# Zero rows that fill the packed remainder of the gate/up products from 96 to 128 rows

## The chip, the cores and the metric

The kernel runs on one core of a Trainium2 chip. A core has five engines that work on their own and meet through semaphores: TensorE (PE, matmuls; PEld is its weight load), VectorE (DVE), ScalarE (ACT), GpSimd (POOL) and SyncE (SP, which only issues transfers here). Each takes its instructions in the order in which the program puts them. The metric is the time of one execution on the device in microseconds; lower is better.

## What is computed

One transformer block over 2048 tokens of 576 features, in float32. The second half, which the change touches, is a gated feed-forward part with 4608 hidden features:

```python
def _B_ref(x, w_gate, w_up, w_down):
    g = _silu(x @ w_gate)
    u = x @ w_up
    return (g * u) @ w_down

h = _layernorm(x, axis=-1) * (1 + ca) + sa
x = x + ga * _A_ref(h, A_wq, A_wk, A_wv, A_wo, A_beta)
h = _layernorm(x, axis=-1) * (1 + cb) + sb
x = x + gb * _B_ref(h, B_w_gate, B_w_up, B_w_down)
```

`_A_ref` is an attention with 32 heads of 18 features in four segments of 512 tokens, with a memory between segments and the output projection `o @ wo`. The factors `sa` to `gb` come from a small product with the vector `c`.

## The kernel before

**Precision.** A float32 operand is split into a high part that the array takes exactly (`wh`, written by a cast on ACT, L1166) and the rest (`wl`, a subtraction on DVE, L1167). A product is then three matmuls: high by high, low by high, high by low.

**Gate and up.** The feed-forward part runs twice over 1024 tokens (`t`), each time over 18 pairs of hidden tiles (`p`), and for each pair over gate and up (`z`). Such a block, 2 x 2 tiles with 512 tokens, 288 features and 128 hidden features a tile, is formed with seven products instead of eight, on sums and differences of the operands: `y[:, o]` holds the seven activation operands (o from 0 to 6), `O` the seven weight operands (three loaded, four formed by `sum_o`, L1157). That makes 2 x 18 x 2 x 7 = 504 products, each written by `prod` (L1195 to L1203) into one of the PSUM banks A, B, C.

A product has 288 = 2 x 128 + 32 contracted features. The two full blocks take three matmuls each. The 32 left over are packed: `R[z]` (tile `wr`) holds on partitions 0 to 31 the high part, on 32 to 63 the low part, on 64 to 95 the high part again, and `y[:, o, 4]` the high, high and low part. So one matmul over 96 partitions does all three. It is the seventh and last of its product. `prep_r` fills `wr`: at `t` 0 with a cast on ACT (L1151) and a subtraction on DVE (L1152), in two parts (slots 0 to 2 and 3 to 6); at `t` 1 with a load of what `store_r` had kept in DRAM. The activations' packed rows are written by `y_here` or loaded by `load_y`.

**Down.** Between the products PE does the down product of the pair before (`down` L1306, `plain` L1323), six or twelve matmuls of 288 columns at a time.

**The order.** Everything after the attention is written under a manual schedule: each engine's instructions stand as the loops write them. `later` is a list of subtractions that `flush` puts on DVE one step after their casts on ACT. The change lies in the stage between the attention and the feed-forward loop. There PE does the output projection of the last segment, `wo_m` (L729, `pw`): 4 token blocks (i) by 2 halves (h), each half 14 matmuls in 4 portions (c), numbered n = 8 i + 4 h + c. Two PSUM banks take turns for the halves, and `wo_x` (L734, `xr`, on DVE) empties one. Beside these portions the first feed-forward operands are made at fixed n: the lists `SS` (sums `sum_o`, the first four on POOL, the last four on DVE), `HH` (`y_here`) and `WW` (`prep_r` and `prep_w`). Ahead of them POOL forms `ys` (`y_sum`, L1037). Afterwards the loop starts with a load of `wd` (L1174) and of the operand 3 of `y` (L1122), both on SP's queue.

The sums in the order that `SS` gives, and the packed matmul:

```python
d, a, b, op = ((4, 3, 2, ALU.add), (5, 4, 0, ALU.subtract), (3, 0, 3, ALU.subtract), (6, 1, 5, ALU.subtract))[j]
eng.tensor_tensor(o[:, d], o[:, a], o[:, b], op=op)

ops.append((R[z][0:96, SLOT[m]], y[0:96, o, 4]))
```

Of the kernel before, what the change touches and what calls it, by code (L numbers as in the profile page):

```python
# [8 lines left out]
F32R = mybir.dt.float32r  # L9
# [6 lines left out]
P = 128  # L16
# [51 lines left out]
def f32(ap):  # L68
    return ap.bitcast(F32)
# [3 lines left out]
def block(ctx: ExitStack, tc: tile.TileContext, x, wqk, wv, wo, beta, wgu, wd, c, w_mod, out):  # L73
    nc = tc.nc
    def pool(stk, name, bufs=1, **kw):
        return stk.enter_context(tc.tile_pool(name=name, bufs=bufs, reuse_waits="tile", **kw))
# [167 lines left out]
    with ExitStack() as p1:  # L244
# [211 lines left out]
        def proj(s, t):  # L456
            hh, hl, hr = hT[s]
            pp = ps.tile([P, L], F32, tag="p", name="pp", bufs=3)
            mm14(pp, lambda k: wqkh[:, t, k, :], lambda k: wqkl[:, t, k, :], lambda k: hh[k],
                 lambda k: hl[k], lambda: hr, True)  # L460
            f = pb.tile([P, L], F32, tag="pf", name="pf")
            fh = pb.tile([P, L], F32R, tag="fh", name="fh")
            fl = pb.tile([P, L], F32R, tag="fl", name="fl")
            nc.scalar.copy(f, pp)
            split(fh, fl, f)
            k0, k1 = 128 * t, min(128 * t + 128, D)
            if k0 < D:
                n = k1 - k0
                nc.sync.dma_start(kD[s][k0:k1, 0:2, :], f32(fh[:n]).unsqueeze(1).to_broadcast([n, 2, L]))
                nc.sync.dma_start(kD[s][k0:k1, 2, :], f32(fl[:n]))  # L470
            q0, q1 = max(128 * t - D, 0), 128 * t + 128 - D
            if q1 > 0:
                n = q1 - q0
                r = P - n
                nc.sync.dma_start(qD[s][q0:q1, 0:3:2, :], f32(fh[r:]).unsqueeze(1).to_broadcast([n, 2, L]))
                nc.sync.dma_start(qD[s][q0:q1, 1, :], f32(fl[r:]))
                if s > 0:
                    nc.sync.dma_start(qF[s][q0:q1, :], f[r:])
            return f
# [34 lines left out]
        for s in range(NSEG):  # L514
# [12 lines left out]
            for t in QKORD:  # L527
# [4 lines left out]
                f = proj(s, t)  # L532
# [160 lines left out]
    def load_xr(s, i):  # L693
        xr = o3.tile([P, D], F32, tag="xr", name="xr") if s < 3 or i in (0, 3) else xp.tile([P, D], F32, tag="xs", name="xr")
        r = L * s + P * i
        nc.sync.dma_start(xr, x[r:r + P, :])
        return xr

    def wo_r(s, i):
        pt = ps.tile([P, 4, P], F32, tag="x", name="pto", bufs=XB if s < 3 else 4)  # L700
        for kt in range(4):
            nc.tensor.transpose(pt[:, kt, :], ot[s][:, i, 128 * kt:128 * kt + 128], ident)
        pto[s, i] = pt
        oh = o3.tile([P, 4, P], F32R, tag="oh", name="oh")
        ol = o3.tile([P, 4, P], F32R, tag="ol", name="ol")
        oT[s, i] = (oh, ol, load_xr(s, i) if s < 3 else xr3[i])

    def wo_s(s, i):
        nc.scalar.copy(oT[s, i][0], pto[s, i])

    def wo_t(s, i):
        oh, ol, _ = oT[s, i]
        nc.vector.tensor_tensor(ol, pto.pop((s, i)), f32(oh), op=ALU.subtract)
# [3 lines left out]
    def wo_m(s, i, h, c, wb=WB):  # L717
        oh, ol, _ = oT[s, i]
        sl = slice(288 * h, 288 * h + 288)
        if c == 0:  # L720
            wps[0] = ps.tile([P, L], F32, tag="w", name="pw", bufs=wb)
        ops = []
        for k in range(4):
            ops += [(oh[:, k], woh[:, k, sl]), (oh[:, k], wol[:, k, sl]), (ol[:, k], woh[:, k, sl])]
        if s == 3:
            ops = [ops[n] for n in (0, 1, 3, 4, 6, 7, 9, 10, 2, 5, 8, 11)]
        ops += [(orr[s][:, i], woh[:, 4, sl]), (orr[s][:, i], wol[:, 4, sl])]
        for n in range(14 * c // WC, 14 * (c + 1) // WC):
            nc.tensor.matmul(wps[0][:, :288], lhsT=ops[n][0], rhs=ops[n][1], start=(n == 0), stop=(n == 13))  # L729

    def wo_x(s, i, h):
        xr = oT[s, i][2]
        sl = slice(288 * h, 288 * h + 288)
        nc.vector.tensor_tensor(xr[:, sl], wps[0][:, :288], xr[:, sl], op=ALU.add)  # L734
        if h == 1:
            (nc.scalar if (s, i) == (2, 3) else nc.sync).dma_start(xD[s][:, i, :], xr)
# [177 lines left out]
    p4 = ExitStack()  # L914
# [3 lines left out]
    SLOT = {1: 0, 2: 1, 3: 6, 4: 2, 5: 4, 6: 5, 7: 3}  # L918
# [120 lines left out]
    def y_here(j):  # L1039
        o, kb = (4, 6, 2)[j // 3], j % 3  # L1040
        n = P if kb < 2 else 96
        f = ys[:, kb] if o == 4 else yh(1 if o == 6 else 2, kb)
        d = y[:, o, kb if kb < 2 else 4]
        nc.scalar.copy(d[:n], f[:n])
        if kb < 2:
            later.append(lambda: nc.vector.tensor_tensor(y[:, o, 2 + kb], f, f32(d), op=ALU.subtract))
        else:
            later.append(lambda: nc.vector.tensor_tensor(d[64:96], f[64:96], f32(d[64:96]), op=ALU.subtract))
# [76 lines left out]
    O, W, R, RW, DP = {}, {}, {}, {}, {}  # L1125
    later = []

    def flush():
        while later:
            later.pop(0)()  # L1130
# [10 lines left out]
        nc.scalar.dma_start(oD[p][z], O[p, z][:, 3:7, 0:2])  # L1141

    def prep_r(t, p, z, part=0):
        if part == 0:
            R[z] = wrp.tile([P, 7, P], F32R, tag="wr", name="wr")
        r = R[z]
        if t == 1:
            (nc.sync if p or z == 0 else nc.scalar).dma_start(f32(r[0:96]), rD[p][z])
            return
        o, c = O[p, z], slice(0, 3) if part == 0 else slice(3, 7)  # L1150
        nc.scalar.copy(r[0:96, c], o[0:96, c, 2, :])  # L1151
        later.append(lambda: nc.vector.tensor_tensor(r[32:64, c], o[32:64, c, 2, :], f32(r[32:64, c]), op=ALU.subtract))  # L1152

    def sum_o(p, z, j, eng=nc.gpsimd):
        o = O[p, z]
        d, a, b, op = ((4, 3, 2, ALU.add), (5, 4, 0, ALU.subtract), (3, 0, 3, ALU.subtract), (6, 1, 5, ALU.subtract))[j]
        eng.tensor_tensor(o[:, d], o[:, a], o[:, b], op=op)  # L1157
# [4 lines left out]
    def prep_w(p, z, m):  # L1162
        o = O[p, z][:, SLOT[m], 0:2]
        wh = wp.tile([P, 2, P], F32R, tag="wh", name="wh")
        wl = wp.tile([P, 2, P], F32R, tag="wl", name="wl")
        nc.scalar.copy(wh, o)  # L1166
        later.append(lambda: nc.vector.tensor_tensor(wl, o, f32(wh), op=ALU.subtract))  # L1167
        W[z, m] = (wh, wl)
# [26 lines left out]
    def prod(z, m, bank, first):  # L1195
        wh, wl = W.pop((z, m))
        o = ACT_OP[m]
        ops = [(wh[:, k] if a != 1 else wl[:, k], y[:, o, 2 + k if a == 2 else k])
               for k in range(2) for a in range(3)]
        ops.append((R[z][0:96, SLOT[m]], y[0:96, o, 4]))  # L1200
        for n, (a, b) in enumerate(ops):
            nc.tensor.matmul(bank, lhsT=a, rhs=b, start=(first and n == 0), stop=(n == 6),  # L1202
                             skip_group_check=not first)  # L1203
# [138 lines left out]
    with tc.manual_schedule():  # L1342
# [30 lines left out]
        y = yp.tile([P, 7, 5, L], F32R, tag="y", name="y")  # L1373
        tp = pool(p4, "tp")
        opl = pool(p4, "opl")
        wp = pool(p4, "wp", WR)
        wrp = pool(p4, "wrp", 2)
        xr3 = {i: load_xr(3, i) for i in range(3)}
        p5 = ExitStack()
        ys = pool(p5, "ys").tile([P, 3, L], F32, tag="ys", name="ys")  # L1380
# [14 lines left out]
        wo_s(3, 1)  # L1395
        wo_t(3, 1)
        gw = iter(MP[:PF])
        for i in range(4):
            for h in range(2):
                for c in range(WC):  # L1400
                    n = 8 * i + 4 * h + c
                    wo_m(3, i, h, c, 2)
                    if c == 3:
                        wo_x(3, i, h)
                    flush()
                    if n in SS:
                        j = SS.index(n)
                        sum_o(0, j // 4, j % 4, nc.vector if j > 3 else nc.gpsimd)
                    if n in HH:
                        y_here(HH.index(n))  # L1410
                    if n in WW:
                        j = WW.index(n)
                        if j < 2:
                            prep_r(0, 0, 0, j)
                        prep_w(0, 0, next(gw))
                if h == 1 and i < 2:
                    wo_r(3, i + 2)
                    wo_s(3, i + 2)
                    wo_t(3, i + 2)
# [21 lines left out]
        for t in range(2):  # L1441
            for p in range(NPR):
# [16 lines left out]
                for k in range(14):  # L1459
                    z, m = ZM[k]  # L1460
# [22 lines left out]
                    if t:  # L1483
                        if k == 2 + swap:
                            prep_r(1, p, 1)
                        elif not last and k == 9:
                            prep_r(1, nx, 0)
# [40 lines left out]
                    if prev is not None and is_plain(*prev):  # L1528
# [3 lines left out]
                        if CH0[t][k]:  # L1532
                            f = plain(*prev, chunk)
# [20 lines left out]
                    if is_plain(t, p):  # L1554
                        if k in DK[dl // 2]:
                            j = DK[dl // 2].index(k)
# [74 lines left out]
```

## Time and profile before

| | |
|---|---|
| median of 3 runs | 1906.63 us (1906.19 to 1909.42) |
| profiled execution, its own time: first to last instruction | 1906.7 us |
| PE busy | 1870.6 us, 98% |
| DVE busy | 1507.7 us, 79% |
| ACT busy | 933.8 us, 49% |
| POOL busy | 579.1 us, 30%, none after some 1300 us |
| mean granted TensorE clock | 0.998 |
| attention, with the projections | until 637.8 us |
| feed-forward part | from there to the end |

The page gives no other time for the profiled execution than this span. How to read its rows: a group's row names line, engine, operation, the tiles written and read, the count, then busy time, mean ns of one, and the idle time of the engine just before them with what ended it. In a timeline row stand start, duration and the idle time before. A matmul's end is modelled and overlaps the next; the starts are what counts. In a window's row stand the stretch, its length, then the busy time (and count) of PE, PEld, DVE, ACT and POOL, the granted clock, the share of the DMA engines and GB/s. The chain is followed back from the last instruction, at each step to what released it.

### The profile page before, as it was taken

How to read it: one execution, taken by the hardware profiler on the slowest of the kernel's cores; microseconds unless marked ns; L12 is line 12 of the kernel's file. 1: busy time of each engine (PE TensorE's matmuls, PEld its weight loads, DVE VectorE, ACT ScalarE, POOL GpSimd, SP SyncE). 2: the span in 40 equal slices, each digit the busy share in tenths (PEclk: the TensorE clock that was granted, in tenths of full speed). 3: DMA queues.
4: the chain of work that ended last, by engine and by line, in shares of the span. 5: the costliest groups of instructions: out<-in, count | busy, mean ns of one | idle time of the engine just before them, and what ended most of it. 6: DMA issues, size and time to landing. Idle time of an engine off the chain costs nothing.

```text
span 1906.7 us, 30703 instructions
## 1 busy us (share of the span) xinstructions
PE 1870.6 (98%) x10927; PEld 1560.4 (82%) x10927; DVE 1507.7 (79%) x3277; ACT 933.8 (49%) x2060; POOL 579.1 (30%) x783
## 2 busy tenths in 40 slices
PE   7999999999999999999999999999999999999999
PEld 4878866676766788888888888888888888888888
DVE  6566358878886888888888888867888888888887
ACT  1222267768767543454454454444445454454542
POOL 5212236455556545445445435400000000000000
PEclk9999999999999999999999999999999999999999
DMA  6767555446654854554454554477333333333331
GB/s 196 253 216 251 200 191 155 131 137 172 186 159 134 301 204 148 170 190 142 170 188 139 186 162 129 152 258 237 102 124 102 98 103 101 123 102 104 104 106 61
DMA packets 179424, 304.31 MB, mean 160 GB/s; under 512 B 26152, under 2 KB 107688, under 8 KB 177352
## 3 DMA queue, kind: packets, MB, share of 16 engines
q1 hardware_dynamic: 150696, 245.29, 41.2%
q10 hardware_dynamic: 28576, 57.07, 8.4%
q8 instruction: 86, 1.41, 0.3%
q14 instruction: 66, 0.54, 0.1%
HBM read 187.98 MB, written 113.77 MB: 158 GB/s over the span
## 4 chain that ended last, share of the span: by engine, by line
PE 91%; DVE 3%; ACT 2%; DMA 2%; POOL 1%; issue 1%; SPq 0%; ACTq 0%; POOLq 0%; DVEq 0%
PE A L1202 23%; PE pd L1323 13%; PE C L1202 12%; PE pd L1306 9%; PE B L1202 6%; PE pp L99 5%; PE s L599 4%; PE av L619 4%; PE s L182 4%; PE pv L99 3%; PE pw L729 3%; PE pn L800 1%; ACT Pt L602 1%; PE px L640 1%; PE pm L448 1%
## 5 line engine op out<-in xcount | busy, mean ns | idle before, releaser
L1202 PE MATMUL A<-y,wh 128*128 128x512 f32 x1152 | 406.3, 393 | 3.1 <-ACT B L1248 2.5
L187 DVE CUSTOM_DVE_ANT_0 junk<-s,tri 128x256 bf16<-128x256 f32 (+3 forms) x512 | 228.5, 486 | 69.0 <-PE s L182 61.8
L1167 DVE TENSOR_TENSOR wl<-O,wh 128x256 fp32r<-128x256 f32 x504 | 262.1, 525 | 3.4 <-ACT wh L1166 2.9
L1202 PEld LDWEIGHTS A<-y,wh 128*128 128x128 f32 x1152 | 217.1, 188 | 47.0 <-ACT B L1248 3.2
L1202 PE MATMUL A<-y,wl 128*128 128x512 f32 x576 | 226.9, 394 | 0.0
L602 ACT ACTIVATE Pt<-s 128x512 f32<-128x512 f32 (+1 forms) x352 | 187.9, 559 | 70.9 <-PE s L599 66.6
L1157 POOL TENSOR_TENSOR O<-O 128x384 f32<-128x384 f32 x140 | 159.4, 1151 | 175.9 <-DMA O<-in_wgu_dram 73.8
L1311 DVE TENSOR_TENSOR acc<-acc,pd 128x576 f32<-128x576 f32 x216 | 162.3, 752 | 58.7 <-PE pd L1306 52.1
L1202 PE MATMUL C<-y,wh 128*128 128x512 f32 x576 | 203.3, 394 | 2.8 <-DMA y<-yD 2.4
L1166 ACT CAST wh<-O 128x256 fp32r<-128x256 f32 x504 | 196.7, 405 | 0.7 <-issue 0.7
L1323 PE MATMUL pd<-dh,al 128*128 128x288 f32 x640 | 189.0, 295 | 0.0
L1323 PE MATMUL pd<-dh,ah 128*128 128x288 f32 x640 | 188.9, 295 | 0.0
L1323 PE MATMUL pd<-dl,ah 128*128 128x288 f32 x640 | 188.8, 295 | 0.0
L1327 DVE TENSOR_TENSOR acc<-acc,pd 128x576 f32<-128x576 f32 x156 | 116.8, 749 | 87.9 <-PE pd L1323 87.6
L1266 ACT CAST ah<-sg 128x512 fp32r<-128x512 f32 x192 | 119.1, 620 | 86.5 <-DVE sg L1226 80.2
L599 PE MATMUL s<-qs,ks 110*128 110x512 f32 (+2 forms) x384 | 150.0, 407 | 3.7 <-ACT Pt L602 2.4
L182 PE MATMUL s<-ks,qs 108*128 108x256 f32 (+3 forms) x512 | 140.3, 326 | 3.2 <-DVE mx L187 3.1
L1267 DVE TENSOR_TENSOR al<-sg,ah 128x512 fp32r<-128x512 f32 x192 | 134.1, 699 | 8.6 <-ACT ah L1266 8.3
L1306 PE MATMUL pd<-dh,ah 128*128 128x288 f32 x448 | 133.0, 297 | 0.0
L1306 PE MATMUL pd<-dh,al 128*128 128x288 f32 x448 | 132.5, 296 | 0.0
L1306 PE MATMUL pd<-dl,ah 128*128 128x288 f32 x448 | 132.3, 295 | 0.0
L1202 PEld LDWEIGHTS C<-y,wh 128*128 128x128 f32 x576 | 108.5, 188 | 23.8 <-DMA y<-yD 2.8
(361 smaller groups left out, 4404.9 us busy)
## 6 DMA issues: line engine op xcount, KB each, us to landing
O<-in_wgu_dram SPq DMA_DIRECT2D x36, 768.0 KB
oD<-O ACTq DMA_DIRECT2D x36, 512.0 KB
O<-oD SPq DMA_DIRECT2D x36, 512.0 KB
ks<-kD SPq DMA_DIRECT2D x64, 216.0 KB
qs<-qD SPq DMA_DIRECT2D x64, 216.0 KB
O<-in_wgu_dram SPq DMA_DIRECT2D x36, 384.0 KB
rD<-wr ACTq DMA_DIRECT2D x36, 336.0 KB
wr<-rD SPq DMA_DIRECT2D x35, 336.0 KB
```

Source lines behind the costliest of these rows:

```text
L99: nc.tensor.matmul(ps, lhsT=a, rhs=b, start=(k == 0), stop=(k == 13))
L182: nc.tensor.matmul(bank[:, n * (h - h0):n * (h - h0) + n], lhsT=qst[b][0:108, h, 128 * i:128 * i + 128], rhs=kst[b][0:108, h // 2, 0:n], s ...
L187: nc.vector.tensor_tensor_reduce(junk[:, :n], bank[:, n * (h - h0):n * (h - h0) + n], tri[:, L - n:], 1.0, -3e38, op0=ALU.add, op1=ALU.max ...
L599: nc.tensor.matmul(bank[:, n * (g - h):n * (g - h + w)].rearrange("p (a b) -> p a b", a=w), lhsT=kst[u % NB][0:110, g // 2, 128 * j:128 * ...
L602: nc.scalar.activation(pt[:, h:h + per, :n], bank[:, :n * per].rearrange("p (a b) -> p a b", a=per), AF.Exp, scale=SCALE)
L1157: eng.tensor_tensor(o[:, d], o[:, a], o[:, b], op=op)
L1166: nc.scalar.copy(wh, o)
L1167: later.append(lambda: nc.vector.tensor_tensor(wl, o, f32(wh), op=ALU.subtract))
L1202: nc.tensor.matmul(bank, lhsT=a, rhs=b, start=(first and n == 0), stop=(n == 6), skip_group_check=not first)
L1306: nc.tensor.matmul(pd[:, i, :288], lhsT=a[:, tk], rhs=w, start=(k == 0), stop=(k == 2))
L1311: nc.vector.tensor_tensor(o, o, pd[:, :, :288], op=ALU.add)
L1323: nc.tensor.matmul(pd[:, i, :288], lhsT=a[:, tk], rhs=w, start=(k == 0), stop=(k == 5))
```

## The change

`wr` and the operands' packed block are used on all 128 partitions, and rows 96 to 127 of both are set to zero once. As the two `wr` tiles must keep their zero rows, they are two fixed tiles, made once, instead of a rotation of two. The two memsets on `wr` stand on POOL ahead of the loop over the projections' portions; those on `y`, for operands 0 and 1, 2 and 3, 4 and 5, and 6, stand on POOL behind each of the four sums that `SS` puts there. The transfers and casts still write 96 rows.

```diff
     def prep_r(t, p, z, part=0):
-        if part == 0:
-            R[z] = wrp.tile([P, 7, P], F32R, tag="wr", name="wr")
         r = R[z]
...
-        ops.append((R[z][0:96, SLOT[m]], y[0:96, o, 4]))
+        ops.append((R[z][:, SLOT[m]], y[:, o, 4]))
...
-        wrp = pool(p4, "wrp", 2)
+        wrp = pool(p4, "wrp")
+        for z in range(2):
+            R[z] = wrp.tile([P, 7, P], F32R, tag=f"wr{z}", name="wr")
...
         gw = iter(MP[:PF])
+        nc.gpsimd.memset(f32(R[0][96:128]), 0.0)
+        nc.gpsimd.memset(f32(R[1][96:128]), 0.0)
         for i in range(4):
             for h in range(2):
                 for c in range(WC):
...
                     if n in SS:
                         j = SS.index(n)
                         sum_o(0, j // 4, j % 4, nc.vector if j > 3 else nc.gpsimd)
+                        if j < 4:
+                            nc.gpsimd.memset(f32(y[96:128, 2 * j:min(2 * j + 2, 7), 4]), 0.0)
                     if n in HH:
                         y_here(HH.index(n))
```

## The prediction

> **What bounds the kernel now.** I read the page first (span, busy shares, the chain that ended last), then two long windows of the feed-forward part, then the chain in order of time around its start, and last single engines there.
>
> ```profile
> span 1906.7 us, 30703 instructions
> ...
> PE 1870.6 (98%) x10927; PEld 1560.4 (82%) x10927; DVE 1507.7 (79%) x3277; ACT 933.8 (49%) x2060; POOL 579.1 (30%) x783
> ...
> PE 91%; DVE 3%; ACT 2%; DMA 2%; POOL 1%; issue 1%; SPq 0%; ACTq 0%; POOLq 0%; DVEq 0%
> ...
> L1202 PE MATMUL A<-y,wh 128*128 128x512 f32 x1152 | 406.3, 393 | 3.1 <-ACT B L1248 2.5
> ...
> L1157 POOL TENSOR_TENSOR O<-O 128x384 f32<-128x384 f32 x140 | 159.4, 1151 | 175.9 <-DMA O<-in_wgu_dram 73.8
> ```
>
> PE is busy for 98% and carries 91% of the chain. All sums below are made against this execution's span of 1906.7 us, which is 0.07 us above the median of the runs shown, 1906.63. A change of 0.2%, about what a measurement of this kernel can tell from none, is 3.8 us.
>
> ```profile
> 700.00:1300.00 600.00, 599.33 (x3304) 528.33 (x3303) 498.29 (x757) 279.26 (x649) 261.24 (x237) 1.00 0.54 176
> 1300.00:1890.00 590.00, 590.00 (x3172) 516.33 (x3171) 505.61 (x926) 280.84 (x650) 0.00 (x0) 1.00 0.34 107
> ```
>
> The second figure is PE's busy time: 599.33 us of 600 and 590.00 of 590, at full granted clock. Behind 700 us PE never waits. So anything that shortens a matmul there is earned in full, and whatever delays the entry into this stretch is lost in full, since no slack takes it up. The entry is this:
>
> ```profile
> 624.67 0.46 DVE xr L734
> 625.13 1.18 DVE y L1046
> ...
> 627.87 1.25 DVE wr L1152
> ...
> 629.57 0.38 DVE xr L734
> ...
> 630.09 6.14 PE pw L729 x42
> ...
> 638.44 0.37 DVE xr L734
> ...
> 639.33 0.33 SPq L1174
> ...
> 640.20 7.63 DMA y<-yD
> ```
>
> The reader sees the last output projections (`pw`, L729) and the first feed-forward work. From 624.67 to 629.95 the chain lies on DVE, which works in order: splits for the first products (`y`, `wr`, `wl`) stand between two `xr` instructions, and `xr` (L734) is what frees a PSUM bank for the next group of `pw`. PE then runs until the last `xr`, behind which SP issues the load of `wd` and of the fourth operand `y`; that load lands at 647.83, and PE's first C product waits for it.
>
> **Part 1, the six memsets.** The diff puts two memsets of 32x896 (the rows 96 to 127 of both `wr`) on POOL ahead of the sums L1157 on the first `O`, and one of 32x1024 behind each of the first three sums (32x512 behind the fourth). In the built program nothing else moves on any engine; POOL is in order, so what stands behind them waits for them.
>
> ```profile
> 619.55 3.81 POOL L1037 TENSOR_TENSOR ys<-yh,yh 128x512 f32<-128x512 f32 x3
> 623.31 5.40 POOL L1157 TENSOR_TENSOR O<-O 128x384 f32<-128x384 f32 x4
> 643.22 3.39 POOL L1180 TENSOR_TENSOR dr__8785<-dr__8785,gbB 128x576 f32<-128x576 f32 x2 [14.52 <-DMA dr__8785<-in_wd_dram]
> ```
>
> ```profile
> L124 POOL MEMSET qs<- 128x1024 f32 x4 | 3.7, 949 | 1.8 <-PE pp L99 1.8
> ...
> L786 POOL MEMSET pq<- 64x512 f32 x3 | 1.6, 520 | 0.0
> ...
> L129 POOL MEMSET tri<- 128x512 f32 x1 | 0.5, 525 | 0.0
> ```
>
> POOL forms `ys`, runs the four sums without a gap until 628.71, and is then free until 643.22, where it had waited for a transfer. For the price: 1024 elements took 949 ns, 512 took 525 ns on 128 partitions and 520 on 64, so the number of partitions does not count, and an element costs (949 - 525) / 512 = 0.83 ns. 896 elements are 949 - 128 x 0.83 = 843 ns. Ahead of the end of the fourth sum stand 2 x 0.843 + 3 x 0.949 = 4.53 us. The last memset, 0.5 us, ends near 634, nine microseconds before the wait for the transfer would end and well before the first matmul that needs it: it costs nothing, and with that cover gone 0.5 us. The fourth sum makes a slot that the second half of `wr` is cast from:
>
> ```profile
> 626.12 0.51 ACT L1151 CAST wr<-O 96x384 fp32r<-96x384 f32 x1
> ...
> 628.74 0.62 ACT L1151 CAST wr<-O 96x512 fp32r<-96x512 f32 x1 [1.81 <-POOL O L1157]
> 629.26 0.40 ACT L1166 CAST wh<-O 128x256 fp32r<-128x256 f32 x1
> ```
>
> ```profile
> 629.97 0.68 DVE L1152 TENSOR_TENSOR wr<-O,wr 32x512 fp32r<-32x512 f32 x1
> ...
> 631.63 0.45 DVE L734 TENSOR_TENSOR xr<-pw,xr 128x288 f32<-128x288 f32 x1
> ```
>
> ```profile
> 632.13 0.40 PE L729 MATMUL pw<-woh,oh 128*128 128x288 f32 x1
> ```
>
> ACT already waits here: 1.81 us idle before the cast of `wr` at 628.74, released by POOL's sum. So the cast moves by the whole 4.53 us, to 633.27, and everything queued behind it on ACT with it (`wh`, `y`, the casts of `oh` for the last token block). DVE's split of `wr` at 629.97 had the cast ready since 629.36; of the delay 629.97 - 629.36 = 0.61 us is slack, and 3.92 us remain. Behind that split, in order, stands the `xr` of 631.63, now at 635.55. PE's group at 632.13 follows its end (631.63 + 0.45) by 0.05 us, because it takes over that bank. So PE stops at 632.1 and goes on at 632.13 + 3.92 = 636.05. DVE has no idle time to catch up with, as the window of 632 to 636 below shows (busy 3.92 of 4 us); the last `xr`, SP's issue of 639.33 and the landing of `y` all move by 3.92. From there to 672 one wait hands over to the next (`y`, then weights, then POOL's sums on them), all started by the shifted work. **Term 1: +3.92 us.** Below, the sums may run faster while DVE stands still (they took 5.40 / 4 = 1.35 us each beside it, 1.15 in the kernel's mean), and the shift is 3.3. Above, they wait for each memset to end, some 0.1 us each: 4.5. Nothing here can gain.
>
> The memsets of `wr` also wait until the stores that used this memory have landed. ACT's cast of the first half of `wr`, at 626.12, needs the same memory and did not stand out with a wait, so I take no cost; a late store would add up to 626.1 - 623.4 = 2.7 us.
>
> **Part 2, the clock after the new pause.** PE gets a pause of 3.92 us that it hasn't now. What a shorter one does is in the trace:
>
> ```profile
> 647.88 0.50 PE L1202 MATMUL C<-y,wh 128*128 128x512 f32 x1 [2.39 <-DMA y<-yD]
> ```
>
> ```profile
> 632.00:636.00 4.00, 4.00 (x30) 3.80 (x29) 3.92 (x9) 1.46 (x4) 0.00 (x0) 1.00 0.72 263
> ...
> 644.00:648.00 4.00, 1.61 (x8) 1.02 (x7) 3.90 (x4) 3.84 (x8) 3.92 (x4) 1.00 0.99 346
> 648.00:652.00 4.00, 4.00 (x11) 3.13 (x12) 1.07 (x3) 0.38 (x1) 1.44 (x2) 0.57 1.05 354
> ```
>
> ```profile
> 647.88 2.90 PE C L1202 x7
> 650.78 2.18 PE A L1202 x7
> ...
> 672.50 1.61 PE B L1202 x7
> ```
>
> PE was busy 1.61 us of 644 to 648, with a pause of 2.39 us, and in the next 4 us the granted clock was 0.57: the C product took 2.90 us where seven matmuls take 1.61. Counted over C and the A product behind it (650.78 to 652.96, 2.18 us) that is 1.29 + 0.57 = 1.86 us. If the new pause brings such a stretch down upon the `pw` groups behind 636, it costs between 0 (the pause falls across two of the clock's intervals, or DVE's chain hides it) and 1.86. I take 1.0, near the middle, since a pause longer than that one of 2.39 us speaks for a slow stretch and DVE's pace for partial cover. **Term 2: +1.0 us.** The Trainium skill ("TensorE: Matmul & The Clock Gate", Part 1) describes a gate that watches free-running intervals of about 3.4 us and halves the clock after an idle one; the 0.57 agrees, and by its figure half an interval, 1.7 us, would be lost as an estimate. That is the rule that speaks against this change.
>
> **Part 3, 504 matmuls of 128 rows instead of 96.**
>
> ```profile
> L1202 PE MATMUL A<-y,wh x1152: 387/389/628, 637.9 to 1887.9; 128*128 128x512 f32 x192
> ...
> L1202 PE MATMUL A<-y,wl x576: 387/393/628, 638.1 to 1887.7; 128*128 128x512 f32 x192
> ...
> L1202 PE MATMUL A<-y,wr x288: 391/397/402, 639.3 to 1888.1; 96*128 96x512 f32 x144
> ...
> L1202 PE MATMUL C<-y,wr x144: 391/397/628, 650.2 to 1889.8; 96*128 96x512 f32 x144
> ...
> L1202 PE MATMUL B<-y,wr x72: 395/397/399, 643.5 to 1881.7; 96*128 96x512 f32 x72
> ```
>
> ```profile
> L99 PE MATMUL pp<-hr,wqkl 128*128 128x512 f32 x36 | 14.2, 395 | 0.0
> ```
>
> The columns are least, median and greatest ns. 288 + 144 + 72 = 504 matmuls have 96 rows. Their median of 397 is 4 above that of the `wl` matmuls and 8 above that of `wh`, which have 128. These differences bound the gain by nearest rows: 504 x 8 ns = 4.0 us, 504 x 4 = 2.0. But the `wr` is also the last of its group, whose end releases others. The nearest row to that is the last matmul of the projections, same 512 columns, 128 rows: 395 ns on average. Against it 2 ns are left, 504 x 2 = 1.0 us. Below, rows may cost nothing: 0; a loss is not excluded, since a fuller array is more work, and I bound it by the same 2 ns, 1.0 us. **Term 3: -1.0 us**, from the row nearest in position, between +1.0 and -4.0. The weight loads stay as they are: they overlap. The Trainium skill (same page, "Why this matters for your kernels") says that a single matmul on 32 rows takes as long as one on 128. By that term 3 is zero and the sum 1911.6, still the forecast's case and counted in its chance; the 397 beside 395 nearly agrees.
>
> `wr` now is two fixed tiles instead of a rotation of two, in use alike: each stays with one `z`. No wait of ACT, DVE or SP changes in the built program; three early matmuls also wait for POOL, for memsets done several microseconds before. Sizes of transfers stay. Cost: nothing; without that cover, the 0.5 us above.
>
> **Sum:** 1906.7 + 3.92 + 1.0 - 1.0 = 1910.6 us, 0.2% slower, at the edge of what can be told.
>
> **The rivals.**
>
> *Delay and gain cancel.* The 397 is a cost of the row count itself, so the gain is 504 x (4 to 8) ns, 2 to 4 us, and the clock isn't lowered: 1906.7 + 3.92 - 3.0 = 1907.6. For it: `wr` is the slowest kind in all three banks. Against it: the 395.
>
> *Faster.* One place, the change of row count between `wr` and what follows: if the array has to settle at each change, the neighbours pay as well. The `wh` matmuls take 393 ns in the mean (the page's row above), the least 387. If `wr` fell to 387 and the six others of its product by 2 ns each, 10 + 12 = 22 ns x 504 = 11.1 us: 1906.7 + 4.9 - 11.1 = 1900.5. It decides from (4.9 + 3.8) / 504 = 17 ns per product. Against it: nothing in the row of `wr` itself shows more than 10.
>
> *The delay is hidden.* If PE had its banks in time, only term 3 would be left, 1905.7. The chain above, with `wr` L1152 in it, speaks against; I count it with the second case.
>
> **How the numbers follow.** Forecast, slower by over 0.2%: 0.5 (own range 1909.5 to 1912.6: both clock ends, term 1 from 3.3 to 4.5). Cancelled or hidden, within 0.2%: 0.3. Faster by over 0.2%: 0.2. The range must reach into the faster case: from 1901.0, which leaves out its lower half, 0.1, to 1913.0 (1906.7 + 4.5 + 1.86, little gain), above which lies under 0.1 with a late store.
>
> **What would show it.** POOL's fourth sum on the first `O` ends near 633.2 instead of 628.71; ACT's wait before the cast of `wr` grows from 1.81 to about 6.3; PE has a wait of some 3.9 us near 632 for DVE `xr`; the granted clock behind 636 falls below 1. The median of `wr` matmuls stays within 395 to 397. Wrong it is if that median falls to 389 or the product of seven falls clearly below 1.61 us, or if the pause on PE is missing.

## The result

| | before | after |
|---|---|---|
| median of 8 runs each | 1906.93 us | 1902.96 us |
| lowest to highest | 1906.19 to 1910.04 | 1900.49 to 1906.84 |
| profiled execution, first to last instruction | 1906.7 | 1900.5 |

The ratio of the times is 0.9974, with a 95% interval of 0.9964 to 0.9984: 5.0 us faster (3.1 to 6.9); the medians lie 4.0 us apart. The forecast was 1910.6 us and slower; the range held the time, the direction was wrong.

The page of the changed kernel:

```profile
span 1900.5 us, 30716 instructions
...
PE 1862.9 (98%) x10927; PEld 1559.2 (82%) x10927; DVE 1509.0 (79%) x3277; ACT 933.8 (49%) x2060; POOL 584.4 (31%) x789
...
PE 90%; DVE 3%; DMA 2%; ACT 2%; POOL 1%; issue 1%; SPq 0%; ACTq 0%; DVEq 0%; POOLq 0%
```

PE is still the engine that sets the end. Its waits in front have grown, and yet the span is shorter, so the time was won behind them.

**The front.** POOL's timeline, then ACT's and DVE's around the cast of `wr` (now L1149 and L1150):

```profile
618.27 3.82 POOL L1037 TENSOR_TENSOR ys<-yh,yh 128x512 f32<-128x512 f32 x3
622.14 0.84 POOL L1398 MEMSET wr<- 32x896 f32 x1
...
623.85 1.48 POOL L1155 TENSOR_TENSOR O<-O 128x384 f32<-128x384 f32 x1
625.38 0.95 POOL L1412 MEMSET y<- 32x1024 f32 x1
...
630.60 0.99 POOL L1155 TENSOR_TENSOR O<-O 128x384 f32<-128x384 f32 x1
```

```profile
624.83 0.51 ACT L1149 CAST wr<-O 96x384 fp32r<-96x384 f32 x1
...
631.62 0.62 ACT L1149 CAST wr<-O 96x512 fp32r<-96x512 f32 x1 [5.97 <-POOL O L1155]
```

```profile
627.62 0.44 DVE L734 TENSOR_TENSOR xr<-pw,xr 128x288 f32<-128x288 f32 x1
632.27 0.68 DVE L1150 TENSOR_TENSOR wr<-O,wr 32x512 fp32r<-32x512 f32 x1 [4.21 <-ACT wr L1149]
...
640.85 0.46 DVE L734 TENSOR_TENSOR xr<-pw,xr 128x288 f32<-128x288 f32 x1 [1.73 <-PE pw L729]
```

The two memsets on `wr` and the first three on `y` stand where the prediction put them, at 0.84 and 0.95 us. The fourth sum ends 13.32 us after `ys` began (618.27 to 631.59), where it had been 9.16 (619.55 to 628.71): 4.16 us later. ACT waits 5.97 us instead of 1.81, DVE 4.21 where it had not waited, and PE, in the view of its waits between 600 and 720 us, once for 4.1 us:

```profile
PE pw L729 <- DVE xr L734: 4.4, 2, 4.1
PE C L1200 <- DMA y<-yD: 2.5, 1, 2.5
```

What this wait costs is told by the place at which PE goes on:

```profile
634.43 0.61 PE L729 MATMUL pw<-woh,oh 128*128 128x288 f32 x1 [4.14 <-DVE xr L734]
```

That is 16.16 us after the start of `ys`, where the same matmul had stood at 12.58 (632.13 - 619.55): 3.6 us later. The wait is longer than that because PE came to it 0.6 us earlier.

The windows (stretch, length, busy time of PE, PEld, DVE, ACT and POOL, then the granted clock) show the second step, too:

```profile
628.00:632.00 4.00, 2.09 (x14) 1.88 (x14) 0.06 (x1) 0.38 (x1) 3.72 (x5) 1.00 1.01 345
632.00:636.00 4.00, 1.57 (x6) 1.57 (x7) 3.70 (x8) 4.00 (x11) 0.17 (x1) 0.62 0.57 207
636.00:640.00 4.00, 4.00 (x20) 4.00 (x19) 2.21 (x5) 0.33 (x1) 0.00 (x0) 0.52 0.17 65
640.00:644.00 4.00, 4.00 (x28) 3.65 (x26) 3.15 (x8) 0.00 (x0) 0.00 (x0) 1.00 0.08 29
```

From 632 to 640 the clock was 0.62 and 0.52, where the kernel before had 1.00; the trace's record of the granted clock has 0.5 from 632.99 to 639.82. Most of the projection matmuls in there start 0.24 us apart instead of 0.13, and the 42 of them from PE's restart to the first product take 8.1 us instead of 5.8, which is 2.3 us more. DVE now waits for PE (1.73 us before the `xr` of 640.85). From the start of `ys` to the first product it takes 642.5 - 618.3 = 24.2 us, before 637.9 - 619.6 = 18.3: the front costs 5.9 us, 3.6 by the delay and 2.3 at the lower clock.

**The stretch that PE fills.** The rows of the product matmuls (least, median, greatest ns, then first and last start):

```profile
L1200 PE MATMUL A<-y,wh x1152: 387/389/628, 642.5 to 1881.5; 128*128 128x512 f32 x192
...
L1200 PE MATMUL A<-y,wl x576: 387/389/628, 642.8 to 1881.3; 128*128 128x512 f32 x192
...
L1200 PE MATMUL A<-y,wr x288: 388/396/398, 643.9 to 1881.7; 128*128 128x512 f32 x144
...
L1200 PE MATMUL C<-y,wr x144: 388/392/628, 654.6 to 1883.3; 128*128 128x512 f32 x144
...
L1200 PE MATMUL B<-y,wr x72: 389/396/398, 648.1 to 1875.4; 128*128 128x512 f32 x72
```

From the first to the last `A<-y,wh` it is 1239.0 us, before 1250.0: 11 us less. The packed matmuls themselves have hardly changed, 396, 392 and 396 ns against 397. More has changed at their neighbours of 128 rows: the median of `wl` is 389, before 393. The chain in order of time shows whole products and down groups. Before:

```profile
1504.61 1.62 PE B L1202 x7
1506.23 0.81 PE pd L1306 x6
1507.04 1.62 PE A L1202 x7
1508.66 1.61 PE pd L1306 x12
```

After, the same places of the loop:

```profile
1501.51 1.59 PE B L1200 x7
1503.10 0.80 PE pd L1304 x6
1503.90 1.59 PE A L1200 x7
1505.49 1.58 PE pd L1304 x12
```

These two products of seven take 1.59 us instead of 1.62, twelve down matmuls 1.58 instead of 1.61. Not every product gains: the C product that follows takes 1.62 in both. The durations of single matmuls hardly show where the time is won, since their ends are modelled; the starts do. From the starts in the two traces I worked out the mean distance from each matmul of a product to the next one, leaving out the first 60 products and the last eight:

| ns from this start to the next | wh | wl | wh | wh | wl | wh | wr | sum |
|---|---|---|---|---|---|---|---|---|
| before | 236 | 234 | 228 | 230 | 229 | 227 | 236 | 1621 |
| after | 232 | 228 | 229 | 229 | 227 | 227 | 232 | 1604 |

Only 4 of the 17 ns are won at the packed matmul. Ten are won at the first two matmuls of a product; the remaining 4 of 21 ns per product, given below, are won in the down matmuls. Where a product follows the last packed matmul directly, as 118 of these 436 do, the loss lies right behind the change: its first three distances are 238, 233 and 231 ns before and 228, 228 and 227 after. Where six down matmuls lie between (160 products), the first two are 231 and 236 before, 229 and 229 after.

For the runs below I give one number beside the time, worked out in the same way: the **filled stretch**, from the start of the 31st product to the last matmul of the 504th. It holds 474 products and lies wholly behind the front. Before it is 1182.0 us, after 1172.0, that is 21 ns per product. Some single waits for transfers and other engines are still in it, and they differ from trace to trace. So I also give the **stretch without waits**: where a distance between starts is more than 40 ns above the usual (227 ns for a product's matmul, 133 for the others), the excess is left out. That concerns 14 to 20 of some 6400 distances. Before it is 1179.6 us, after 1169.6.

### The profile page after: what moved, and what is told of

The parts are those of the page before. It is cut to its first block, busy times and chain, and to the rows that moved or that the text cites. A ratio compares the mean times of both kernels' runs of the same rounds, so it can differ in the third digit from the quotient of the medians.

```text
span 1900.5 us, 30716 instructions
## 1 busy us (share of the span) xinstructions
PE 1862.9 (98%) x10927; PEld 1559.2 (82%) x10927; DVE 1509.0 (79%) x3277; ACT 933.8 (49%) x2060; POOL 584.4 (31%) x789
## 4 chain that ended last, share of the span: by engine, by line
PE 90%; DVE 3%; DMA 2%; ACT 2%; POOL 1%; issue 1%; SPq 0%; ACTq 0%; DVEq 0%; POOLq 0%
PE A L1200 23%; PE pd L1321 13%; PE C L1200 12%; PE pd L1304 9%; PE B L1200 6%; PE pp L99 6%; PE s L599 4%; PE av L619 4%; PE s L182 4%; PE pv L99 2%; PE pw L729 2%; PE pn L800 1%; PE px L640 1%; ACT Pt L602 1%; PE pm L448 1%
```

## The experiments

Two theories stood against each other at first. *Row change*: PE loses time whenever consecutive matmuls differ in their number of rows, and the memsets cost 5 to 6 us in front. *Bookkeeping*: the fixed `wr` tiles made the difference. Where a version was measured once, its stretch tells more than its time. Every diff is against the changed kernel or the one named.

### e1: 96 rows again, with the memsets kept

```diff
-        ops.append((R[z][:, SLOT[m]], y[:, o, 4]))
+        ops.append((R[z][0:96, SLOT[m]], y[0:96, o, 4]))
```

> The changed kernel with its memsets and its two fixed wr tiles, but the packed matmul on 96 rows again. Row-change theory (the gain comes from PE no longer changing its row count, the memsets cost 5 to 6 us in front): median of wr 397 ns, first to last A wh product 1250 us as in the kernel before, time 1911 to 1914, slower than before by 5 to 6. Bookkeeping theory (the fixed tiles, not the rows, made the products shorter): first to last stays at 1239 and the time near 1903.

Measured: 1912.71 us against 1905.56 for the kernel before on the same chip, ratio 1.0033 (1.0020 to 1.0045), so 6.3 us slower (3.8 to 8.6). The filled stretch is 1181.5 us, without waits 1179.7. The rows of the products:

```profile
L1200 PE MATMUL A<-y,wh x1152: 387/389/628, 643.4 to 1892.7; 128*128 128x512 f32 x192
...
L1200 PE MATMUL A<-y,wr x288: 391/397/403, 644.8 to 1892.9; 96*128 96x512 f32 x144
```

1249.3 us from first to last and 397 ns: the whole gain is gone with the 128 rows, though the fixed tiles are still there, and the front's cost stays. Bookkeeping falls.

### e2: the memsets behind the four sums

```diff
-        nc.gpsimd.memset(f32(R[0][96:128]), 0.0)
-        nc.gpsimd.memset(f32(R[1][96:128]), 0.0)
...
                         sum_o(0, j // 4, j % 4, nc.vector if j > 3 else nc.gpsimd)
-                        if j < 4:
-                            nc.gpsimd.memset(f32(y[96:128, 2 * j:min(2 * j + 2, 7), 4]), 0.0)
+                        if j == 3:
+                            nc.gpsimd.memset(f32(R[0][96:128]), 0.0)
+                            nc.gpsimd.memset(f32(y[96:128, :, 4]), 0.0)
+                            nc.gpsimd.memset(f32(R[1][96:128]), 0.0)
```

> The changed kernel, 128 rows, with all memsets on POOL behind the four sums instead of ahead of and between them. Theory that the memsets delay ACT's cast of wr and through it DVE and PE: ACT's wait before that cast is back at about 1.8 us, PE's 4.1 us wait for DVE xr is gone, the granted clock near 636 stays 1.00, and the time is 5 to 6 us below the changed kernel: 1896 to 1898. If the entry is long for another reason: 1902 to 1903.

Measured: 1897.23 us, ratio to the kernel before 0.9955 (0.9942 to 0.9969). ACT's cast, PE's waits between 600 and 720 us, and the products:

```profile
629.24 0.62 ACT L1149 CAST wr<-O 96x512 fp32r<-96x512 f32 x1 [1.84 <-POOL O L1155]
```

```profile
PE C L1200 <- DMA y<-yD: 2.2, 1, 2.2
...
PE pw L729 <- DVE xr L734: 0.9, 1, 0.9
```

```profile
L1200 PE MATMUL A<-y,wh x1152: 387/389/792, 638.4 to 1877.6; 128*128 128x512 f32 x192
...
L1200 PE MATMUL A<-y,wr x288: 387/396/404, 639.8 to 1877.9; 128*128 128x512 f32 x144
```

ACT waits 1.84 us again, PE 0.9 for `xr`, and the products keep their 1239.2 us (filled stretch 1171.5, without waits 1169.5). The granted clock is 1.00 from 632 to 644 us. So the delay came from where the memsets stood in POOL's order, and the gain can be had without it. The version is faster than the kernel before. In the trace the front is back to its old length, 18.4 us from `ys` (620.0) to the first product (638.4), as the kernel before with 18.3; that is the gain of 5 to 6 us that was expected. The times show less of it: against the changed kernel's 0.9974 the ratio is lower by 3.6 us, that of a second measurement, below (0.9952), by 4.2, and both intervals still touch that of the changed kernel (0.9964 to 0.9984).

### e3: 112 rows

Against e2, as all that follow:

```diff
-        ops.append((R[z][:, SLOT[m]], y[:, o, 4]))
+        ops.append((R[z][0:112, SLOT[m]], y[0:112, o, 4]))
```

> As e2, but the packed matmul reads 112 rows of both operands (rows 96 to 111 are zero). If what counts is that the number of rows is equal, 112 costs what 96 did: first to last A wh product 1249 to 1251, time about 1907. If what counts is which of the four blocks of 32 rows are in use, 112 is as good as 128: first to last about 1239, time about 1897.

Measured once: 1911.29 us; filled stretch 1183.1, without waits 1179.6.

```profile
L1200 PE MATMUL A<-y,wh x1152: 387/389/628, 636.4 to 1890.5; 128*128 128x512 f32 x192
...
L1200 PE MATMUL A<-y,wr x288: 391/397/403, 637.8 to 1890.8; 112*128 112x512 f32 x144
```

```profile
PE C L1200 <- DMA y<-yD: 5.0, 1, 5.0
```

397 ns, and the stretch without waits is that of 96 rows, though 112 rows touch all four blocks of 32. So what counts isn't which blocks are in use. The time lies above the expected 1907 since this run's front was longer: PE waited 5.0 us for the operand `y` instead of 2.2. 1254.1 us from first to last hold that wait, the filled stretch doesn't.

### e6: 96 rows everywhere

All product and down matmuls read rows 0 to 95 only:

```diff
         ops.append((R[z][:, SLOT[m]], y[:, o, 4]))
+        ops = [(a[0:96], b[0:96]) for a, b in ops]
...
-                nc.tensor.matmul(pd[:, i, :288], lhsT=a[:, tk], rhs=w, start=(k == 0), stop=(k == 2))
+                nc.tensor.matmul(pd[:, i, :288], lhsT=a[0:96, tk], rhs=w[0:96], start=(k == 0), stop=(k == 2))
```

(and the same in `plain`)

> As e2, but every matmul of the feed-forward products and of the down products reads rows 0 to 95 alone; the rows 96 to 127 of each contraction are left out, so this shows time and nothing else. Theory that the change of the row count costs: no change is left, so as fast as 128 throughout, first to last about 1239, time about 1897. Theory that a matmul of 96 rows is itself slower than one of 128: all are slow, first to last above 1250, time above 1907.

Measured once: 1901.35 us; filled stretch 1173.1, without waits 1169.5.

```profile
L1201 PE MATMUL A<-y,wh x1152: 387/389/643, 637.7 to 1880.6; 96*128 96x512 f32 x192
...
L1201 PE MATMUL A<-y,wr x288: 388/396/632, 639.1 to 1880.8; 96*128 96x512 f32 x144
```

396 ns, and 1242.9 us from first to last with a front a little longer than e2's. A stream of 96 rows alone is as fast as one of 128: the distances between starts are those of the changed kernel, place by place (232, 228, 229, 229, 227, 227, 232 ns). A matmul of 96 rows isn't slow. The change between the two is.

### e5: half of the products

```diff
-        ops.append((R[z][:, SLOT[m]], y[:, o, 4]))
+        n_ = 128 if z == 0 else 96
+        ops.append((R[z][0:n_, SLOT[m]], y[0:n_, o, 4]))
```

> As e2, but only the gate products (z = 0) use 128 rows in the packed matmul, the up products 96. Row-change theory with the effect local to a product: half of the gain, A wh products from first to last about 1244 to 1245 us instead of 1239 or 1250, time about 1902. If one change somewhere keeps the array slow for long after, the gate products stay slow too and first to last is near 1250.

Measured once: 1905.59 us, filled stretch 1179.3.

```profile
L1201 PE MATMUL A<-y,wh x1152: 387/389/628, 637.6 to 1884.8; 128*128 128x512 f32 x192
...
L1201 PE MATMUL A<-y,wr x288: 388/396/401, 639.0 to 1885.0; 128*128 128x512 f32 x72, 96*128 96x512 f32 x72
```

The packed matmuls come in both forms. 1247.2 us from first to last lie between the two outcomes that were expected, and the filled stretch gives back only 2.7 of the 10.5 us between 1182.0 and 1171.5. But that isn't the rows alone. At the start of the second 1024 tokens PE waits for a transfer, which it does neither in the kernel before nor in e2:

```profile
1288.86 0.47 PE L1201 MATMUL A<-y,wh 128*128 128x512 f32 x1 [1.42 <-DMA y<-yD]
```

Without waits the stretch is 1175.2: of the 10.1 us between 1179.6 and 1169.5, 4.4 came back, a little under half of the loss for half of the changes. The starts tell where, if one takes the products that follow another directly and sorts them by the rows of two packed matmuls, the one ahead of the product and its own:

| rows ahead, own | products | sum of the seven distances, ns | the same products before, in e2 |
|---|---|---|---|
| 128, 128 | 25 | 1590 | 1616, 1590 |
| 128, 96 | 31 | 1601 | 1618, 1596 |
| 96, 128 | 46 | 1610 | 1617, 1589 |
| 96, 96 | 16 | 1616 | 1615, 1587 |

With 96 rows ahead, the first distance is 236 to 238 ns instead of 227; with 96 of its own, the packed matmul's is 5 to 6 ns longer. So a change costs the odd matmul a little and the first matmuls behind it more, in the next product, and a product with no change on either side pays nothing. Behind six down matmuls it is less clean: with 128 rows on both sides the sum is 1610 against 1603 in e2.

### e7: two matmuls of 96 rows in each product

```diff
+        ops = ops[:5] + [(a[0:96], b[0:96]) for a, b in ops[5:]]
```

> As e2, but the last two matmuls of each product read 96 rows (rows 96 to 127 of the sixth are left out, time only). As many changes of the row count as in the kernel before, twice as many matmuls of 96 rows. Row-change theory: the cost of the kernel before, some 21 ns per product, first to last about 1250, time about 1907. Theory that each 96-row matmul among 128-row ones costs by itself: 42 ns per product, first to last about 1260, time about 1918.

Measured once: 1909.69 us, filled stretch 1182.0, without waits 1180.2.

```profile
L1201 PE MATMUL A<-y,wh x1152: 387/394/499, 638.3 to 1888.9; 128*128 128x512 f32 x192
...
L1201 PE MATMUL C<-y,wh x576: 387/393/504, 648.3 to 1890.5; 128*128 128x512 f32 x144, 96*128 96x512 f32 x48
```

1250.6 us from first to last, and the C row shows the second kind of matmul with 96 rows (48 of 192 in its first form). The stretch is that of the kernel before within 0.6 us, with twice as many matmuls of 96 rows and as many changes. The cost goes with the change.

### e4: 64 rows

```diff
-        ops.append((R[z][:, SLOT[m]], y[:, o, 4]))
+        ops.append((R[z][0:64, SLOT[m]], y[0:64, o, 4]))
```

> As e2, but the packed matmul reads 64 rows (the third of the three packed products is left out, time only). If any change of the row count costs the same: about 21 ns per product as at 96 and 112 rows, first to last about 1250. If the cost grows with the difference in rows, or 64 switches the array into another mode: clearly more than 1250.

Measured once: 2092.55 us, filled stretch 1361.4. The products, and a piece of PE's timeline:

```profile
L1200 PE MATMUL A<-y,wh x1152: 387/390/793, 634.7 to 2071.2; 128*128 128x512 f32 x192
...
L1200 PE MATMUL A<-y,wr x288: 492/498/502, 636.2 to 2071.5; 64*128 64x512 f32 x144
```

```profile
1502.45 0.39 PE L1200 MATMUL A<-y,wh 128*128 128x512 f32 x1
1502.76 0.50 PE L1200 MATMUL A<-y,wr 64*128 64x512 f32 x1
1503.19 0.40 PE L1304 MATMUL pd<-dh,ah 128*128 128x288 f32 x1
```

(1361.4 - 1171.5) us / 474 = 401 ns per product, nineteen times the cost of 96 or 112 rows. From the packed matmul's start to the next it is 0.43 us, and 0.31 from the matmul ahead of it, where 0.23 is usual. The size speaks for another mechanism. The Trainium skill ("TensorEngine Tiling (Array Packing)", "Available Configurations" and "Key Properties") lists 64 rows as a tiling mode of its own and says that changing the mode drains the engine; the 401 ns agree, though it gives no time for it. It lists none between 64 and 128, and the 21 ns of 96 and 112 rows stand in no such rule. No run has 64 rows throughout, so what a matmul of 64 rows costs by itself isn't separated from the change.

### e8: the change put into the down product

The last matmul of each down group:

```diff
-                nc.tensor.matmul(pd[:, i, :288], lhsT=a[:, tk], rhs=w, start=(k == 0), stop=(k == 2))
+                r_ = 96 if i == 1 and k == 2 else 128
+                nc.tensor.matmul(pd[:, i, :288], lhsT=a[0:r_, tk], rhs=w[0:r_], start=(k == 0), stop=(k == 2))
```

(in `plain` with `k == 5`)

> As e2, with 128 rows in all products, but the last matmul of each down group (288 columns, 384 groups: 224 in L1304's loop, 160 in L1321's) reads 96 rows; rows 96 to 127 of it are left out, time only. Row-change theory as a rule for any matmul: 384 x some 20 ns = 7 to 8 us more than e2, about 1905. If the cost belongs to the 512-column products alone: the time of e2, 1897.

Measured once: 1904.46 us, filled stretch 1179.7, without waits 1176.1.

```profile
L1200 PE MATMUL A<-y,wh x1152: 387/389/628, 637.1 to 1883.7; 128*128 128x512 f32 x192
```

1246.6 us from first to last, and 8.2 us more of filled stretch than 1171.5; but PE waits 1.5 us for a transfer of `y` here, as in e5. Without waits it is 6.6 us over the 368 groups in the stretch, 18 ns each. The cost isn't bound to the packed matmul, its columns or its place.

### e9, e10: equal rows in the attention

The attention's score matmuls have 110 and 108 rows among others of 128. First one and then both were filled with zero rows:

```diff
         nc.gpsimd.memset(f32(qst[b][:, 2:4]), 0.0)
+        nc.gpsimd.memset(f32(kst[b][96:128]), 0.0)
...
-                                 lhsT=kst[u % NB][0:110, g // 2, 128 * j:128 * j + 128],
-                                 rhs=qst[u % NB][0:110, g:g + w, 128 * j:L], start=True, stop=True)
+                                 lhsT=kst[u % NB][:, g // 2, 128 * j:128 * j + 128],
+                                 rhs=qst[u % NB][:, g:g + w, 128 * j:L], start=True, stop=True)
```

> As e2, and the attention's second score matmul (L599) reads 128 rows instead of 110, the added ones zeroed in ks and qs. By the order of e2's matmuls this leaves 660 of 907 changes of the row count in the attention. Row-change theory, if PE sets the pace there: 247 changes fewer by some 20 ns, about 5 us below e2, less where PE waits for other engines: 1892 to 1896. If changes only cost among full 512-column products: as e2, 1897.

and in the second:

```diff
             nc.sync.dma_start(f32(qst[b][r, e:4:2, :]), v[1])
+        if u >= NB:
+            for a in range(2):
+                nc.sync.dma_start(f32(qst[b][108 + a:109 + a]).rearrange("p a t -> p (a t)"), tri[16 * a:16 * a + 16, 0:P])
...
-                                 lhsT=qst[b][0:108, h, 128 * i:128 * i + 128],
-                                 rhs=kst[b][0:108, h // 2, 0:n], start=True, stop=True)
+                                 lhsT=qst[b][:, h, 128 * i:128 * i + 128],
+                                 rhs=kst[b][:, h // 2, 0:n], start=True, stop=True)
```

> As e9, and the first score matmul (L182) reads 128 rows instead of 108 too; for that two small transfers per unit set rows 108 and 109 of qs to zero before it. No change of the row count is left between 250 and 625 us. Row-change theory: 907 changes by up to 20 ns, at most 18 us below e2; since PE waits for ACT and DVE here in part, 1884 to 1893. If changes don't cost there: as e2, 1897, or slower by the added transfers.

with e2 beside them:

> e2 once more, beside e9 and e10 on the same chip: 1896 to 1898.

Measured, ratios to the kernel before: 0.9935 (0.9914 to 0.9955) with one filled, 0.9952 (0.9935 to 0.9969) with both, 0.9952 (0.9937 to 0.9966) with none; medians 1895.28, 1898.75 and 1898.61 us. The product rows tell by their first start when the attention was done (one, both, none):

```profile
L1201 PE MATMUL A<-y,wh x1152: 386/389/796, 636.6 to 1875.9; 128*128 128x512 f32 x192
```

```profile
L1204 PE MATMUL A<-y,wh x1152: 387/389/535, 635.2 to 1876.6; 128*128 128x512 f32 x192
```

```profile
L1200 PE MATMUL A<-y,wh x1152: 387/389/504, 638.1 to 1878.4; 128*128 128x512 f32 x192
```

The first product starts at 636.6, 635.2 and 638.1 us. All 907 changes taken away come with 2.9 us there, 3 ns each, and that is within what single executions of the same attention differ by (634.7 in e4, 638.4 in the first run of e2). Behind the attention nothing differs: the stretch without waits is 1169.6 in all three. The three times can't be told apart. The rule as expected, up to 20 ns per change, failed here. The two added transfers per unit may have taken something back; PE's short matmuls of unequal columns and its waits for ACT and DVE may leave nothing to win. Neither was tried.

## Why the prediction was wrong

- **Term 1, the delay by the memsets (+3.92 us): right, a little large.** Each link was as told: POOL's sum later, ACT's wait, DVE's order, PE's wait for `xr`. The sum came 4.16 us later instead of 4.53, since the sums ran faster while DVE stood still, as the lower bound had allowed (0.99 to 1.01 us for the last three). Less the slack of 0.61 that gives the 3.6 us by which PE went on later. The memsets cost 0.84 and 0.95 us against 0.843 and 0.949. The landing of earlier stores cost nothing, as taken. With the memsets moved, the wait was gone.
- **Term 2, the clock (+1.0, between 0 and 1.86): right in kind, mis-sized.** It measured 2.3 us, above its own bound, and the cover by DVE that I had hoped for didn't come: DVE waited for PE. The clock was at 0.5 for 6.83 us, where the pause of 2.39 us in the kernel before had been followed by 3.41 us (648.43 to 651.84). The 1.7 us that I had worked out from the Trainium skill ("TensorE: Matmul & The Clock Gate", Part 1) are for one interval of about 3.4 us at half the clock; here it was twice as long. The Trainium skill asks for an idle interval of that length ahead of it; in the kernel before, 2.39 us without a matmul were enough. The front alone, with 96 rows, made the kernel slower by 6.3 us (3.8 to 8.6).
- **Term 3, the rows (-1.0, between +1.0 and -4.0): wrong, and this decided the sign.** It came to -10.6 us: 504 times 21 ns. The step that failed is "These differences bound the gain by nearest rows". I bounded the gain by the duration of the packed matmul itself, and that duration hardly moved: 396, 392 and 396 ns, two of the three still within the 395 to 397 named as the sign of being right. The time was lost at its neighbours, above all at the first matmuls of the next product. The `wl` matmuls, which I had used as a control of 128 rows, were no control: their own median fell from 393 to 389 with the change. Nor was the 395 ns of the last projection matmul, since a duration in this view tells little of the distance between starts. By the starts, a product of seven fell from 1.62 to 1.60 us, which is what the prediction had named as the sign of being wrong. The rule that one matmul of few rows takes as long as one of 128 (the Trainium skill, "TensorE: Matmul & The Clock Gate", "Why this matters for your kernels") speaks of a single matmul; in the stream 96 rows alone are as fast, as it says, but 64 among 128 took 401 ns more.
- **The rival "Faster" had the mechanism, and its size came out with some luck.** It asked for a loss at each change that the neighbours share, priced at 22 ns and 11.1 us; measured were 21 ns and 10.6. It decided from 17 ns. But it had put 10 ns on the packed matmul and 2 on each of the six others; the starts give 4 there and the most at the first two of the next product. And the row that it rested on, the mean of 393 ns of the `wh` matmuls against a least of 387, doesn't show the loss: after the change the mean is still 392. "Cancelled" and "hidden" didn't happen.
- **The sum** by measured terms is 3.6 + 2.3 - 10.6 = -4.7 us, against -5.0 (3.1 to 6.9 faster). The prediction's own range for "slower", 1909.5 to 1912.6, doesn't follow from the terms that it names, which give 1909.0 to 1912.1; nothing here hangs on it.
- "Whatever delays the entry is lost in full" and "anything that shortens a matmul there is earned in full" held: the front's cost and the filled stretch's gain both appear at the end. That PE never waits behind 700 us is nearly so: it was 0.7 us for transfers in the kernel before, and some 2 us in e5.

## What to carry to other kernels

Where PE is full and a stream of equal matmuls has one with fewer rows in it, fill that one with zero rows: 96 or 112 among 128 cost about 21 ns in each product here, 64 cost 401. In the attention the same filling won nothing that could be measured. Look at the distance between the starts of all matmuls around the odd one, not at the odd one's duration, and take single waits out before two such stretches are compared. Set the zeros where the engine that sets them has nothing queued that another engine waits for; here that was some 4 of the 9 us that the change is then worth.

## What was not expected of the hardware

- An array fed 96 rows throughout keeps the distances of one fed 128 (stretch without waits 1169.5 and 1169.6 us), and 112 among 128 costs as much as 96 (1179.6 both). So between 96 and 128 neither the number of rows nor the blocks of 32 in use matter, only that neighbours are equal.
- Most of the loss falls behind the odd matmul, not on it: where the next product follows directly, 19 of 25 ns on its first three matmuls. Where six down matmuls lie between, the second matmul of the next product still takes 236 ns instead of 229, while the down matmuls themselves hardly change (132.8 to 132.1 ns in the mean). What in PE keeps such a memory is open. Each of these matmuls has its own weight load with the same number of rows, so no run tells which of the two is disturbed.
- In the attention the same filling gave nothing that could be measured.
